# A hand-ordered attention and channel-mix kernel: the plan of steps is placed anew, with other matmuls on zeros

## The chip, the cores and the metric

The kernel runs on one core of one Trainium2 chip. The metric is device time in microseconds (us) of one execution; the time before is the median of three runs. The core has a matrix engine (PE, with its weight loads listed as PEld), a vector engine (DVE), a scalar engine (ACT), a general engine (POOL) and a queue engine (SP); each executes its own instructions strictly in the order in which they were written, and waits on semaphores for the others. Data moves between HBM and on-chip memory by DMA; matmuls write to PSUM, which has eight banks, numbered 0 to 7 in the plan.

## What is computed

Eight batches of eight heads, 576 tokens, head size 64, 32 memory slots. First an attention over a compressed memory, then a channel mix over the 512 joined features, with a shift by one token:

```python
a = softmax(phi)                              # over the 32 slots
k_m = einsum('bhsm,bhsd->bhmd', a, k)
v_m = einsum('bhsm,bhsd->bhmd', a, v)
attn = softmax(q @ k_m.T / sqrt(64))
x = (attn @ v_m) as [B, S, H * D]             # 8, 576, 512
x_prev = x shifted by one token, 0 in front
xk = mu_k * x + (1 - mu_k) * x_prev
xr = mu_r * x + (1 - mu_r) * x_prev
k = maximum(xk @ w_k, 0)                      # 512 -> 1024
out = sigmoid(xr @ w_r) * (k * k @ w_v)       # 1024 -> 512
```

## The kernel before

All of the work is cut into named steps, and a hand-written list, `PLAN` (lines 19 to 84), says in which order they are written out. A loop at line 794 reads it word by word; every word appends the instructions of its step to the queues of the engines concerned. So the list fixes the order on each engine, and the PSUM banks too. A word is `who:step`, then perhaps `/a` or `/d` (ACT or DVE does the copy or the elementwise work) and `@` with the banks that its matmuls take. A step in several stages appears as often as it has stages: `c3:5@2` writes the first matmuls, `c3:5/a` a copy, `c3:5` the last matmuls. The semaphores follow from the data and from the banks: a step that takes a bank waits until the reader of what lay there is done.

The words that matter here:

- `0:` to `7:` are the attention steps of a batch: `exp` of phi, `z` its sums, `kg`, `vg`, `k`, `v`, `kv` the memory products (L319), `h`, `nk`, `nv` their normalization, `tk`, `vt` transposes (L368, L470), `q0`, `q1` the turning of Q (DVE, L388), `s` the scores (L402), `es` their exponentials (ACT, L416, L420), `l`, `r`, `y` the softmax sums, reciprocals and products of batch 0, `fe`, `fs`, `fo`, `w` the same of the later batches, on DVE.
- Batch 0 forms the mixed rows xk and xr directly: `mk`, `mr` (matmuls, L362) and `uk`, `ur`, which unload them to x0T (L545). Its keys are `c0:` (L599, halves a and b, with relu and square as second and third stage), its gates `g:00` to `g:03` (L666).
- Batches 1 to 7 project the memory values through the weights instead: `G02`, `G01`, `Gs0` and so on (L492), `E` to copy them out of PSUM into G (L498), `D` their differences, `d` the differences of the attention between neighbour tokens. A `G0` step reads weights scaled by mu: `m:k0`, `m:k1` (the two halves of w_k) and `m:r0` (w_r) make those (L287). Their keys are `c1:` to `c7:` (L617, L621, L625), relu `r:`, square `s:`, gates `g:10` and so on (L679, L687), `t:` the gates' tanh (L656); `x:` copies the leftover rows of two batches together, `g:e`, `o:e` treat these.
- `o:` is the value product (L757, eight matmuls, one for each block of the 1024 rows), the multiplication by the gate (DVE, L763) and the store. `o:03a` and `o:03b` are its left and right half of the columns, in batch 0 256 each.
- `p:` issues a load on POOL's queue: `p:v:1` is V of batch 1, `p:wk:4-8` a part of the key weights, `p:wv:2-4` the right half of the columns of the value weights, `p:wr` the gate weights.
- `b:2x8@6` writes matmuls on a tile of zeros whose result nobody reads: two of 8 blocks of 64 columns, into bank 6. `WARM` says how many such matmuls stand in front of everything, and how wide.

Stores go to SP's queue; the steps named in `TAIL` spread theirs over SP's and ACT's queue. PE is written so that matmuls of one batch fill the gaps that another's dependencies leave.

Of the kernel before, what the change touches and what calls it, by code (L numbers as in the profile page):

```python
# [16 lines left out]


PLAN = [
# [64 lines left out]
]  # L84

WARM = (36, 2)

PRE = "after: id: q:0a"
TAIL = ("o:73", "o:70", "o:e3", "o:72", "o:71a", "o:71b",)


NJ = 9
# [5 lines left out]
def kernel(  # L98
# [158 lines left out]

    keep_busy(*WARM)

# [579 lines left out]
```

## Time and profile before

| what | value |
|---|---|
| median of three runs | 192.69 us (192.68, 192.69, 194.08) |
| the profiled execution | 194.68 us, its span 192.6 us |
| busy share of PE, DVE, ACT, POOL | 95%, 82%, 79%, 15% |
| mean granted PE clock | 0.988 |
| bytes moved by DMA | 31.91 MB, mean 166 GB/s |

A page of the profile lists busy time by engine, then 40 slices of the span with busy shares and the granted clock of PE in tenths, the DMA queues, the chain of work that ended last (followed back from the last instruction through whatever released each step), and groups of instructions by line. In a group's row stand the line, the engine, the operation, output and input tiles with shapes and the count; behind the bar the busy time in total, the mean ns of one, and then the idle time just before them with what ended it. Instructions that follow each other on an engine overlap a little, so that a group's busy time over its count is less than the mean of one.

### The profile page before, as it was taken

How to read it: one execution, taken by the hardware profiler on the slowest of the kernel's cores; microseconds unless marked ns; L12 is line 12 of the kernel's file. 1: busy time of each engine (PE TensorE's matmuls, PEld its weight loads, DVE VectorE, ACT ScalarE, POOL GpSimd, SP SyncE). 2: the span in 40 equal slices, each digit the busy share in tenths (PEclk: the TensorE clock that was granted, in tenths of full speed). 3: DMA queues.
4: the chain of work that ended last, by engine and by line, in shares of the span. 5: the costliest groups of instructions: out<-in, count | busy, mean ns of one | idle time of the engine just before them, and what ended most of it. 6: DMA issues, size and time to landing. Idle time of an engine off the chain costs nothing.

```text
span 192.6 us, 6111 instructions
## 1 busy us (share of the span) xinstructions
PE 182.2 (95%) x2492; PEld 104.3 (54%) x2492; DVE 158.1 (82%) x341; ACT 151.3 (79%) x360; POOL 29.5 (15%) x45
## 2 busy tenths in 40 slices
PE   7888898999999999999989999999999999999991
PEld 6435663468755466555644565465534753566450
DVE  2147788699988999999997899998999899949441
ACT  2756679797679989999989979978698898587600
POOL 5844242210430140000064000000000000000000
PEclk9999997999999999999999999999999999999998
DMA  5999999999999999992439999724023304413063
GB/s 181 282 203 239 231 207 203 293 241 229 222 231 326 246 225 268 289 192 64 109 33 267 229 241 242 159 49 94 3 58 80 83 12 100 95 44 82 0 163 109
DMA packets 25755, 31.91 MB, mean 166 GB/s; under 512 B 2168, under 2 KB 20352, under 8 KB 25728
## 3 DMA queue, kind: packets, MB, share of 16 engines
q0 software_dynamic: 17888, 20.32, 56.7%
q1 hardware_dynamic: 6272, 8.79, 17.7%
q10 hardware_dynamic: 1568, 2.43, 3.7%
q8 instruction: 19, 0.31, 0.6%
q14 instruction: 8, 0.07, 0.1%
HBM read 38.28 MB, written 9.44 MB: 248 GB/s over the span
## 4 chain that ended last, share of the span: by engine, by line
PE 85%; DMA 5%; ACT 3%; DVE 2%; issue 2%; POOL 1%; POOLq 0%; DVEq 0%; ACTq 0%
PE pv L757 33%; PE pk L625 7%; PE pk L617 7%; PE pb L625 7%; PE gps L492 5%; DMA kv<-in_v_dram 5%; PE pr L687 3%; PE pr L679 3%; PE pb L687 3%; PE kvps L319 3%; PE pr L666 3%; PE pk L599 3%; PE pr L709 2%; PE scps L402 2%; ACT rl L583 1%
## 5 line engine op out<-in xcount | busy, mean ns | idle before, releaser
L757 PE MATMUL pv<-wv,sq 128*128 128x512 bf16 (+3 forms) x296 | 60.8, 350 | 0.0
L757 PEld LDWEIGHTS <-sq 128*128 128x128 bf16 x296 | 27.8, 98 | 26.1 <-issue 3.0
L498 ACT CAST G<-gps 128x512 bf16<-128x512 f32 x63 | 33.6, 618 | 2.1 <-PE gps L492 1.0
L763 DVE SCALAR_TENSOR_TENSOR o<-sg,pv 128x512 f32<-128x512 f32 (+3 forms) x41 | 25.0, 615 | 8.2 <-PE pv L757 7.4
L625 PEld LDWEIGHTS <-G 128*128 128x128 bf16 x224 | 21.5, 98 | 9.1 <-issue 0.6
L625 PE MATMUL pk<-diff,G 128*128 128x288 bf16 x112 | 22.9, 286 | 0.0
L625 PE MATMUL pb<-diff,G 128*128 128x288 bf16 x112 | 22.9, 286 | 0.0
L583 ACT ACTIVATE rl<-pb 128x288 bf16<-128x288 f32 x41 | 17.2, 422 | 6.9 <-PE pb L625 6.7
L583 ACT ACTIVATE rl<-pk 128x288 bf16<-128x288 f32 (+2 forms) x45 | 18.1, 420 | 2.8 <-PE pk L625 1.3
L617 PE MATMUL pk<-atn,G 128*128 128x288 bf16 x112 | 20.0, 286 | 0.0
L621 ACT COPY pb<-pk 128x288 f32<-128x288 f32 x39 | 14.8, 413 | 5.1 <-PE pk L617 1.8
L589 ACT ACTIVATE sq<-rl 128x576 bf16<-128x576 bf16 (+2 forms) x29 | 18.4, 655 | 0.2
L591 DVE TENSOR_TENSOR sq<-rl 128x576 bf16<-128x576 bf16 (+2 forms) x43 | 17.1, 412 | 1.6 <-ACT rl L583 0.9
L501 DVE TENSOR_TENSOR G<-G 128x1024 bf16<-128x1024 bf16 x21 | 14.1, 685 | 0.3
L498 DVE CAST G<-gps 128x512 bf16<-128x512 f32 x21 | 13.8, 683 | 0.6 <-PE gps L492 0.6
L465 DVE TENSOR_TENSOR atn<-e,lz 128x576 bf16<-128x576 bf16 (+2 forms) x18 | 12.1, 683 | 2.5 <-ACT lz L437 2.5
L617 PEld LDWEIGHTS <-G 128*128 128x128 bf16 x112 | 10.4, 98 | 5.6 <-issue 1.1
L656 ACT ACTIVATE sg<-pr 128x512 f32<-128x512 f32 x22 | 13.0, 617 | 0.5 <-PE pr L709 0.5
L585 DVE TENSOR_SCALAR rl<-pk 128x288 bf16<-128x288 f32 (+2 forms) x27 | 11.9, 449 | 1.7 <-PE pk L599 1.2
L388 DVE STREAM_TRANSPOSE qT<-q 128x576 uint32<-128x576 uint32 (+2 forms) x16 | 12.1, 764 | 1.3 <-DMA q<-in_q_dram 1.3
L174 POOL DMA_DIRECT2D kv<-in_v_dram x7 | 5.2, 749 | 37.6 <-PE gps L492 28.5
L299 ACT ACTIVATE em<-ph 128x1152 bf16<-128x1152 f32 (+1 forms) x9 | 9.6, 1075 | 1.6 <-DMA ph<-in_phi_dram 1.6
(99 smaller groups left out, 290.6 us busy)
## 6 DMA issues: line engine op xcount, KB each, us to landing
out_dram<-o SPq DMA_DIRECT2D x51, 128.0 KB, 2.4
ph<-in_phi_dram POOLq DMA_DIRECT2D x7, 576.0 KB, 14.2
kv<-in_k_dram POOLq DMA_DIRECT2D x7, 576.0 KB, 18.5
q<-in_q_dram POOLq DMA_DIRECT2D x7, 576.0 KB, 17.2
kv<-in_v_dram POOLq DMA_DIRECT2D x7, 576.0 KB, 16.3
out_dram<-o SPq DMA_DIRECT2D x26, 64.0 KB, 4.8
k0f<-in_k_dram ACTq DMA_DIRECT2D x2, 576.0 KB, 5.9
wv<-in_moe_w_v_dram POOLq DMA_DIRECT2D x2, 512.0 KB, 18.4
```

What stands on the lines that cost most here:

```text
L388: nc.vector.transpose(dst, src)
L498: return lambda: copier()(g_tile()[:, v, c, GCOLS[i]], st["gps", v, i][c])
L501: return lambda: nc.vector.tensor_sub(g_tile()[:, 1, :, GCOLS[i]], g_tile()[:, 2, :, GCOLS[i]], g_tile()[:, 0, :, GCOLS[i]])
L583: nc.scalar.activation(rl, ps, AF.Relu, scale=HALF ** 0.5)
L589: nc.scalar.activation(dst, rl, AF.Square)
L591: nc.vector.tensor_mul(dst, rl, rl)
L617: nc.tensor.matmul(pa, lhsT=st["G"][:, 2, c, f], rhs=st["at"][:, c, :NP], start=c == 0, stop=False, skip_group_check=True)
L621: copier()(pb, pa)
L625: nc.tensor.matmul(ps, lhsT=st["G"][:, v, c, f], rhs=st["d"][:, kind, c], start=False, stop=c == 1, skip_group_check=True)
L656: nc.scalar.activation(gated[name], ps, AF.Tanh, scale=0.5)
L757: nc.tensor.matmul(pv[:, cols], lhsT=squares, rhs=wv_sb[:, fi, cols], start=(fi == 0), stop=(fi == NF - 1))
L763: nc.vector.scalar_tensor_tensor(o[:, cols], in0=gated[name][:, cols], scalar=1.0, in1=pv[:, cols], op0=AL.add, op1=AL.mult)
```

## The change

All 64 lines of the plan are replaced. The same steps stand in both, apart from the `b:` words; their order, banks and engines differ. Zeros: 36 matmuls in 18 words for 20 in 10. Nearly all of the old ones stand ahead of the keys of batch 0; the new ones also stand within the keys, between the mixing of the gates' rows and the scores of batch 1 (`b:1x6@2`, `b:1x8@7`, `b:1x6@6`) and behind `1:vt`. In front, 10 matmuls of 512 columns take the place of 36 of 128. `p:wv:2-4` is issued ahead of `p:v:1`, `p:q:1` ahead of `p:phi:1` and `p:k:1`. The half values `o:02b`, `o:03b`, `o:01b`, `o:00b` stand ahead of `1:vt` (before, behind it); `m:r0` goes from DVE to ACT, `m:k0` to behind `1:s`. `TAIL` names the last three steps in place of the last six. Nothing but these three constants is changed.

```diff
 PLAN = [
-    "0:exp0 0:mub@0 0:mub 0:c00/a 0:exp1 b:6x8@6 b:1x7@6 0:z@0 p:q:0b 0:c01/a 0:z 0:c11/a 0:c10/a 0:mu@1 p:v:0g 0:q0",
-    "0:kg0@02 b:2x8@6 b:1x7@6 0:kg1 0:h0/d 0:h1/a b:2x8@6 0:tk@0 0:tk p:v:0h 0:q1 p:wk:4-8 p:wk:2-4 p:wk:0-2 0:mu",
-    "p:phi:1 p:k:1 p:q:1 p:wr:0-4 b:1x5@6 0:s0@0234 0:es10 b:2x8@6 0:l10@1 p:v:1 p:wv:2-4 p:wv:0-2 p:phi:2 0:es00",
-    "0:l00@5 0:l10 0:l00 0:r10 0:y10 0:s1@6702 0:r00 0:es01 b:2x8@1 0:vg1@34 0:vg0 0:y00 0:es11 0:nk0 0:l11@0 0:nk1",
-    "0:l01@2 0:l11 0:mk0@6715 0:uk00/d 0:uk01/a 0:nr1 0:l01 0:r01 0:y01 b:2x8@0 b:1x7@0 c0:4a@0 c0:6a@1 0:r11",
-    "c0:5a@2 c0:3a@5 c0:6a/a c0:7a@1 c0:4a/d 0:nr0 0:y11 0:mk1@3406 c0:7a/d m:k0/d 0:uk10/a c0:4a/d c0:0a@7 c0:6a/d",
-    "c0:2a@1 c0:1a@0 c0:0a/d 0:uk11/a c0:4b@3 c0:7a/a c0:7b@4 c0:4b/d 1:exp c0:7b/d c0:4b/a m:k1/d c0:0a/a c0:5b@7",
-    "c0:2a/a c0:5b/a c0:2a/d c0:7b/d c0:0b@3 c0:6b@4 c0:1b@1 c0:5b/d 1:z@6 c0:3b@7 c0:1b/d c0:1b/d c0:6b/a c0:3a/a",
-    "c0:3a/a c0:6b/d c0:2b@5 1:z c0:5a/a p:phi:3 c0:3b/a 0:mr1@1462 c0:0b/a c0:0b/d c0:5a/a p:k:2 0:ur10/a c0:2b/a",
-    "1:k@73 1:q0 1:nk/a c0:3b/d c0:2b/d 0:ur11/a 1:q1 0:mr0@1653 1:tk@7 1:tk c0:1a/a c0:1a/d 1:s@7024 0:ur00/a x:0/a",
-    "1:es0 0:ur01/d g:00@1 1:es1 m:r0/d g:01@3 g:02@5 0:tb g:00 1:fe 1:v@60 1:fs 1:nv/a g:01 g:02 g:03@2 1:vt@0",
-    "1:vt/d 1:G02@06 1:fo g:03 1:G01@47 1:E011/a 1:Gs0@13 1:E020/d p:v:2 o:03b@2 o:03b 1:Es00/a 1:Es01/a 1:E021/a",
-    "1:w0 1:E010/a o:00b@5 1:G00@20 1:E001/a 1:Gs1@13 1:Es11/a 1:w1 1:Gs2@67 1:Es20/a 1:E000/a o:00b o:01a@4",
-    "1:Es21/a 1:d c1:2@5 c1:1@0 c1:0@3 c1:1/a@2 o:01a c1:3@4 o:03a@6 1:D0 c1:2/a@7 c1:2 1:Es10/d o:03a 1:D1 c1:1",
...
-    "c7:1@2 c7:7/a@0 g:70@3 r:700/d g:71/d@6 c7:1/a@5 c7:7 r:701/d s:74/d g:70/d@7 c7:1 r:710/d s:76/a s:70/a g:71",
-    "r:711/a s:71/d t:711 r:770/a g:70 g:e3@2 t:700 t:710 r:771/d t:701 g:e3 s:77/d o:73@1 o:70@5 x:7/a o:73 o:70",
-    "o:e3@0 o:72@1 o:e3 o:72 o:71a@0 o:71a o:71b@1 o:71b",
+    "0:exp0 0:mu@0 0:mub@1 0:mub 0:c01/a 0:c11/d 0:c00/a 0:exp1 b:11x8@6 b:1x7@6 0:z@1 0:z 0:c10/a 0:kg0@23 0:kg1",
+    "0:mu 0:h0/d 0:h1/d b:2x8@6 b:1x7@6 0:tk@0 0:q0 0:tk b:2x8@6 b:1x7@6 0:s0@0123 p:q:0b p:v:0h p:v:0g 0:q1",
+    "p:wk:0-2 p:wk:4-8 p:wk:2-4 0:es10 0:es00 b:3x8@6 0:l10@4 0:l10 0:l00@5 0:l00 0:r10 0:y10 0:s1@6701 0:es11",
+    "0:es01 0:r00 b:2x8@4 b:2x8@5 0:l11@0 0:l01@1 0:vg1@67 0:y00 0:l11 0:l01 p:q:1 b:1x8@5 0:vg0 0:nk1 0:nk0 b:2x8@5",
+    "b:1x7@5 0:mk0@2301 0:uk01/d p:phi:1 0:r11 0:nr1 0:nr0 0:r01 0:y01 0:uk00/a b:2x8@5 c0:1a@4 c0:0a@0 c0:0a/a",
+    "c0:1a/a c0:7a@6 p:k:1 c0:4a@7 c0:5a@0 p:wr:0-4 0:y11 c0:0a/d c0:2a@1 c0:1a/a c0:4a/a c0:6a@2 c0:5a/a c0:6a/a",
+    "0:mk1@0347 c0:3a@5 0:uk11/a m:k1/d c0:6a/a c0:4a/d 0:uk10/d c0:5a/a b:1x5@2 c0:5b@2 c0:3b@0 p:wv:2-4 c0:7a/d",
+    "c0:7a/d c0:3a/d c0:2a/a c0:2b@1 c0:1b@5 1:q1 c0:0b@6 c0:2a/a p:v:1 c0:3a/a c0:3b/a 1:q0 c0:4b@0 1:exp c0:5b/d",
+    "c0:3b/d c0:5b/d p:wv:0-2 c0:7b@2 c0:6b@3 c0:2b/a c0:4b/a 1:z@0 p:phi:2 c0:0b/a c0:2b/d c0:4b/d c0:1b/a c0:6b/a",
+    "c0:0b/d c0:7b/d 1:z c0:6b/d c0:1b/a c0:7b/d x:0/d 0:mr1@1456 1:k@37 0:ur11/d 0:ur10/a b:1x6@2 0:mr0@0215 1:nk/a",
+    "1:tk@3 1:tk 0:ur01/a b:1x8@7 b:1x6@6 1:s@3725 m:k0/d 0:ur00/a 1:es0 1:es1 g:02@0 g:01@1 g:03@2 1:fe 1:fs 0:tb",
+    "g:00@3 o:02b@5 1:fo p:v:2 1:w0 o:03b@7 g:03 g:02 o:02b o:03b o:01b@4 m:r0/a 1:v@60 g:00 p:k:2 p:q:2 g:01",
+    "o:00b@5 p:phi:3 1:nv/a p:v:3 1:w1 1:vt@0 1:vt/d o:01b b:1x8@3 1:G01@06 o:00b 1:G00@71 1:Gs0@42 1:E000/d",
+    "1:E011/a 1:Es00/a 1:Gs1@53 1:d o:01a@6 1:Es01/a c1:1@2 c1:3@4 o:01a 1:Es10/d c1:2@7 c1:0@6 1:Es11/a o:00a@3",
+    "1:E001/a c1:3/a@1 p:k:3 1:E010/a 1:D0 c1:0/d@5 c1:3 c1:2/d@0 o:00a 2:exp c1:0 c1:2 r:100/d r:130/a r:101/a",
+    "s:10/d r:120/a r:131/a c1:6@3 1:D1 o:02a@4 r:121/a c1:6/a@6 c1:5@7 c1:7@0 c1:7/a@1 s:12/d s:13/a c1:6 c1:5/d@5",
...
+    "c7:1/d@2 r:701/d s:70/a o:62 c7:1 c7:3/d@6 g:70@7 c7:2 r:710/a c7:3 g:70/a@3 r:731/a r:720/a g:70 c7:7@0",
+    "r:711/a r:730/d g:71@1 s:71/d g:71/a@6 s:73/a g:e3@2 r:721/d s:72/a c7:7/d@4 c7:7 r:771/d r:770/d s:77/d g:71",
+    "t:711 g:e3 t:700 o:70@4 o:70 o:73@0 x:7/a o:e3@2 o:73 o:72@0 o:e3 o:71a@2 o:71b@4 t:710 t:701 o:72 o:71a o:71b",
 ]
 
-WARM = (36, 2)
+WARM = (10, 8)
 
 PRE = "after: id: q:0a"
-TAIL = ("o:73", "o:70", "o:e3", "o:72", "o:71a", "o:71b",)
+TAIL = ("o:72", "o:71a", "o:71b",)
```

92 rows, old and new, of the table PLAN are left out of this document.

## The prediction, made before the new kernel was run

> **What bounds the kernel now.** I read the page first: busy time by engine, then the slices with the granted clock.
>
> ```profile
> span 192.6 us, 6111 instructions
> ...
> PE 182.2 (95%) x2492; PEld 104.3 (54%) x2492; DVE 158.1 (82%) x341; ACT 151.3 (79%) x360; POOL 29.5 (15%) x45
> ...
> PEclk9999997999999999999999999999999999999998
> ```
>
> PE, the matrix engine, is busy for 95% of the span: the plan is one queue of matmuls with little air. But 95% is an average, and the clock row has a seventh slice that is not full. I then asked for busy time in stretches.
>
> ```profile
> 17.73:31.27 13.54, 11.84 (x229) 8.32 (x228) 10.58 (x33) 10.30 (x30) 5.37 (x7) 1.00 1.22 229
> ```
> ```profile
> 38.00:83.00 45.00, 44.96 (x697) 28.07 (x711) 42.99 (x90) 40.11 (x97) 7.48 (x10) 1.00 1.18 254
> ```
> ```profile
> 27.75:31.17 3.42, 2.75 (x123) 1.59 (x122) 2.48 (x7) 3.42 (x12) 1.47 (x2) 1.00 1.22 205
> 31.17:34.58 3.41, 3.31 (x39) 1.24 (x40) 3.11 (x10) 3.39 (x8) 0.74 (x1) 0.50 1.45 199
> 14.10:17.50 3.40, 2.55 (x94) 1.39 (x94) 2.25 (x7) 2.25 (x10) 0.74 (x1) 1.00 1.33 199
> ```
>
> After the length the columns are busy us of PE, weight loads (PEld), DVE, ACT and POOL, then the clock, the DMA share and GB/s. From 38 us on PE has no gap (44.96 of 45), with DVE (42.99) close behind. Ahead of that lies a prologue paced by batch 0 and by the loads. In 31.17 to 34.58 PE is busy for 3.31 us, but at a clock of 0.50: this follows 3.4 us in which it ran small tiles alone. Third, the chain of waits (start, length, what), cut to the places that the sum needs:
>
> ```profile
> 5.16 9.64 DMA kv<-in_v_dram
> 14.84 0.83 PE kvps L319 x72
> ...
> 16.06 0.67 PE mxps L362 x16
> ...
> 17.73 2.34 PE pk L599 x20
> ...
> 31.27 0.71 PE scps L402 x30
> 31.97 4.00 PE pr L666 x12
> 35.97 0.68 PE kvps L319 x72
> 36.65 0.97 PE pr L666 x4
> ...
> 37.99 0.84 PE gps L492 x24
> 38.83 1.85 PE pv L757 x16
> ...
> 64.73 1.73 PE pv L757 x8
> ```
>
> V of batch 0 lands and starts the mixing (mk0, 16.06), the mixed rows start the keys (17.73), those lead to the scores of batch 1 (31.27), then come gates and the transposed V of batch 1 (vt), and from 37.99 PE is saturated. The real matmul work is the same in both plans. So three things decide: when the new plan saturates PE, how much real work it has done by then, and how well it feeds PE afterwards.
>
> **How the runs stand to this execution.** It took 194.68 us for a span of 192.6, so 2.1 lie around the span. The timed runs are 192.68, 192.69 and 194.08. The half-clock stretch has a price: twelve gate matmuls of 512 columns took 4.00 us, while eight value matmuls of that width take 1.73, so twelve should take 2.59; that is 1.41 lost. The slow timed run is 1.39 above the other two. I read this as: two runs of three had no half-clock stretch, and 192.69 is a time without it. The profiled execution, with it, is 1.99 above the median; the other 0.6 I leave to profiling. What that means for this change: the drop can be removed only from runs that have it, and the median has none.
>
> [...]
>
> **The change, part by part.**
>
> *Ten wide zeros for 36 narrow ones, and a longer row of zeros before the softmax sums of batch 0.*
>
> ```profile
> 5.46 1.87 PE L254 MATMUL idle<-zeros 128*128 128x512 bf16 x7
> ```
>
> Seven zeros of nearly full width take 1.87 us with the end of the last, 0.22 each. Ten end at 1.0+2.2 = 3.2 us, before PE waits for mu anyway (first matmul on it at 4.85). Eleven and one of 7/8 take 2.6 from about 5.5, so end at 8.1; the sums wait for the second exp of phi, which sits one cast (0.67) later in ACT's queue than before, at about 8.6. Cost nothing; were the cover gone, 0.2. In all the plan has 36 zeros for 20: 17,728 columns for 9,856, in front 5,120 for 4,608, so 8,384 columns more, 3.5 us at 0.216 per 512. That is the ceiling if none were covered.
>
> *Ahead of the keys.* The second half of the score exponentials and their sums now stand before V of batch 0, and V's two halves are separate steps with a zero between.
>
> ```profile
> 13.76 0.82 ACT L437 ACTIVATE lz<-lz 128x320 f32<-128x320 f32 x2
> 14.48 0.77 ACT L420 ACTIVATE e<-scps 128x128 bf16<-128x128 f32 x4
> 16.79 0.65 ACT L545 CAST x0T<-mxps 128x256 bf16<-128x256 f32 x2 [0.57 <-PE mxps L362]
> ```
>
> New order on ACT: one reciprocal (0.41), then the four exponentials (0.77): done at 14.95. PE waits for them, does two sums and both halves of V with a zero: 16.1, where before V's sums ended at about 15.6. Behind that, two scalings on DVE, and on PE 0.62 us of zeros that mostly run under them: mk0 at about 16.8 instead of 16.06, keys at 18.4. **Term 1: +0.7** (from 0, if the load of V holds the old order too, to +1.0).
>
> *Keys to the scores of batch 1.* Before: 13.54 us with ACT busy 10.30 and DVE 10.58, so 3 us of air from mutual waits. The new order takes the scaling of the first half of the key weights (m:k0, four by 0.35, 1.4) off DVE and puts it behind the scores; DVE gets two unloads of the mixed rows (0.8 each) and fewer squares, ACT one unload less and more relus. By the steps' counts ACT comes to about 10.8, DVE to 10.0. Following banks and engines word by word I come to 13.0 us. Zeros of 5, 6, 8 and 6 blocks (0.67) lie in waits for an unload or for the normed keys. **Term 2: -0.5**; ends 10.8 (ACT without air, -2.7) and 13.8 (ACT with all the old air, +0.3).
>
> *Loads.* The order on POOL's queue changes.
>
> ```profile
> 30.03 0.74 POOL L174 DMA_DIRECT2D q<-in_q_dram  x1 [1.55 <-DMA wr<-in_moe_w_r_dram]
> 33.12 0.74 POOL L174 DMA_DIRECT2D kv<-in_k_dram  x1 [2.35 <-DMA kv<-in_v_dram]
> ```
>
> Each issue waits for an earlier transfer, so these rows tell landings: gate weights 30.0, V of batch 1 at 33.1, 3.1 us for 576 KB. Half of the value weights (512 KB) put between them lands at about 32.7 and V at 35.8. Values are wanted at 35.5 and V at about 38 in the new order: covered. Q of batch 1 moves ahead of phi and K, which land 3 us later (about 25 and 28); the exponential wants phi at 25.3, K is wanted at 28.7. Cost nothing, with 0.3 to spare on phi; if phi is late ACT waits as long.
>
> *Scores to vt.* Here four half values of batch 0 move ahead of vt: by the row of 16 matmuls in 1.85, 3.7 us of real work done earlier. But m:r0 moves from DVE to ACT, between the gates' tanh steps and the scaled V.
>
> ```profile
> L656 ACT ACTIVATE sg<-pr 128x512 f32<-128x512 f32 x4 | 2.2, 606 | 0.0
> L416 ACT ACTIVATE e<-scps 128x288 bf16<-128x288 f32 x4 | 1.3, 439 | 0.0
> L296 ACT ACT_TABLE_LOAD x1 | 1.3, 1283 | 0.0
> L650 ACT COPY rest<-sq 128x512 bf16<-128x512 bf16 x1 | 0.7, 734 | 0.0
> L353 ACT ACTIVATE vb<-kvps,rz 128x64 bf16<-128x64 f32 x2 | 0.5, 312 | 1.4 <-PE kvps L319 1.4
> ```
>
> No row shows ACT scaling 512 columns of weights. Nearest are the tanh, 0.55 each in a row, and the copy with 0.73: four are 2.2 to 2.9; I take 2.4, nearer to the pipelined row. ACT's queue from the scores: an unload 0.7, exponentials 1.3, table 1.3, four tanh 2.2, m:r0 2.4, V's scaling 0.5, then transpose and copy 0.7: 9.2, with hand-overs 9.4. PE's own work there is 0.4+3.5+3.7+0.7 = 8.3, so ACT sets the end. Before it was 37.99-31.27 = 6.72, without the half clock 5.31. So +4.1, less 3.7 done ahead. **Term 3: +0.4** (-0.7 if PE sets the end, +0.9 with the slow copies). K0's scaling and DVE's sums run beside it; the zero after vt (0.22) runs under its copy.
>
> *Behind saturation.* The tail runs the same six values. Stores of three of them go to SP's queue alone, but eight issues there end before the last value needs one. What differs is the mix:
>
> ```profile
> L498 ACT CAST G<-gps 128x512 bf16<-128x512 f32 x63 | 33.6, 618 | 2.1 <-PE gps L492 1.0 <-PE pr L709 0.8
> ```
>
> In the first 43 us of matmul work from vt I count 94 ACT and 83 DVE steps, 87 and 79 before. At 33.6/63 = 0.53 each that is 3.7 us more on ACT and 2.1 on DVE, in a stretch where they were busy for 40.1 and 43.0 of 45. Most only moves ahead. **Term 4: +0.3** (-0.5, as waits on ACT now on the chain may fall away, to +3.7).
>
> **Sum.** 0.7-0.5+0.4+0.3 = +0.9: 193.6 on the median of 192.69. On the profiled execution: 192.6-1.4+0.9 = 192.1 span, 194.2 with what lies around it.
>
> **Rivals.** *ACT and DVE become the bound in batches 1 to 3.* The filler that fed PE there, four half values, is spent; each c-step needs its G cast and difference. For: DVE 42.99 of 45 already; the counts. Against: PE had no gap with the old mix, and later stretches have slack. It decides once more than 2 us of the added 3.7 plus 2.1 reach PE; with half of it, 2.9: 192.69+0.6+2.9 = 196.2; with 1.7, 195.0. Chance 0.30.
>
> *The half clock belongs to the median after all and the zeros end it, and the keys tighten.* For: zeros stand in the very stretch that preceded the drop. Against: 194.08 beside 192.69. Then 192.69-1.41+0.9 = 192.2; with term 2 at -2.2, 190.5. Chance of that last case, 0.22.
>
> *The zeros don't do it:* the 0.5 us of them (16% of 3.41) are fewer than the 0.6 us of zeros (two of 512 columns, one of 448) in the window 14.10 to 17.50, which kept its clock. If the new plan drops in most runs: 193.6+1.4 = 195.0. Chance 0.05.
>
> **How the numbers follow.** Forecast, near the old time, 0.43. 1% is 1.9 us, about what can be told from no change: below 190.8 is faster, above 194.6 slower. Faster 0.22, same 0.43, slower 0.35. The range goes from 190.6 (term 2 at its good end) to 196.2 (first rival); the likeliest case alone spans 191.9 to 194.6.
>
> **What would show it.** Keys start at 18.1 to 18.7; scores of batch 1 at 30.5 to 32; G of batch 1 at 40 to 42 with ACT full before it; clock 1.00 in the slice at 31 us; PE gaps of over 1 us between 42 and 85 would show the first rival. G of batch 1 before 39.5, or a median difference equal to the lost 1.41, would make me wrong.

## The result, and the profile after

The changed kernel takes 191.67 us, the median of 20 runs (191.32 to 194.22), against 193.16 us for the kernel before on the same chip (20 runs, 192.33 to 194.55). The ratio is 0.9909, 95% interval 0.9884 to 0.9934; it leaves out runs more than 1.5% above a kernel's fastest (two of after), while the medians hold all runs. The forecast was 0.9 us slower; the median came out 1.5 us lower, still within 1%. First the page of after: span, engines, clock by slice.

```profile
span 189.6 us, 6095 instructions
...
PE 183.6 (97%) x2482; PEld 103.4 (55%) x2482; DVE 155.7 (82%) x335; ACT 153.2 (81%) x366; POOL 29.5 (16%) x45
...
PEclk9999999999999999999999999999999999999998
```

The slice at half clock is gone, and the span is 3.0 us shorter. But the profiled execution of before had that stretch and many of its runs don't. So the fair partner is a second profile of before without it (the run `before_again`, the same code; span 191.4). Busy time by stage, columns as in the prediction; the stages are first key to scores of batch 1, scores to G of batch 1, and from there on. First `before_again`, then after:

```profile
17.76:31.50 13.74, 11.84 (x227) 8.32 (x226) 10.66 (x33) 10.27 (x30) 5.29 (x7) 1.00 1.22 228
31.50:36.71 5.21, 4.78 (x120) 2.37 (x123) 4.70 (x12) 5.18 (x13) 1.48 (x2) 1.00 1.43 221
36.71:82.30 45.59, 45.15 (x705) 28.36 (x714) 43.60 (x92) 40.54 (x98) 7.46 (x10) 1.00 1.17 258
```
```profile
18.15:30.18 12.03, 11.90 (x247) 8.37 (x252) 10.61 (x34) 10.29 (x30) 4.00 (x6) 1.00 1.24 230
30.18:38.83 8.65, 8.55 (x154) 5.37 (x155) 7.29 (x14) 7.85 (x17) 1.70 (x3) 1.00 1.28 238
38.83:83.00 44.17, 44.12 (x691) 26.79 (x692) 42.57 (x92) 41.68 (x99) 9.43 (x13) 1.00 1.16 251
```

PE's air in the key stage fell from 1.90 us to 0.13, and the stage from 13.74 to 12.03. Some 0.6 of PE's 11.90 are zeros that fill waits: without them (the run `after_no_late_same_count` below) the stage takes 12.01 with PE busy for 11.27. Behind G PE stays full, with ACT at 41.68 and DVE at 42.57 of 44.17. The chain of waits of after (start, length, what) has the same steps at other times:

```profile
17.26 0.35 PE mxps L362 x16
...
18.15 3.24 PE pk L599 x28
...
30.18 0.41 PE scps L402 x25
30.59 3.56 PE pr L666 x16
34.15 2.62 PE pv L757 x24
36.77 0.68 PE kvps L319 x72
37.45 0.98 PE pv L757 x8
38.43 0.10 PE vtps L470
...
38.83 0.46 PE gps L492 x8
```

The 2.62 and 0.98 of value matmuls (pv) between scores and G are the work done ahead. Stage by stage, after less `before_again`:

| stage | before_again | after | difference | forecast |
|---|---|---|---|---|
| start to first key | 17.76 | 18.15 | +0.39 | +0.7 |
| first key to scores | 13.74 | 12.03 | -1.71 | -0.5 |
| scores to G, less 3.7 done ahead | 5.21 | 8.65 | -0.26 | +0.4 |
| G to end, plus those 3.7 | 154.69 | 150.77 | -0.22 | +0.3 |
| span | 191.4 | 189.6 | -1.80 | +0.9 |

These are two executions out of kernels whose runs spread: 193.45 lies high among the shorter runs of before, 191.42 low among those of after, so that -1.80 is more than the medians show. The start moves most: another profile of the changed kernel (`after_again`) has its first key at 18.94. The three later stages repeat to 0.1 there.

### The profile page after: what moved, and what is told of

It reads as the page before. It is cut to its first block, busy times and chain, and to the rows that moved or that the text cites. A ratio compares the mean times of both kernels' runs of the same rounds, so it can differ in the third digit from the quotient of the medians.

```text
span 189.6 us, 6095 instructions
## 1 busy us (share of the span) xinstructions
PE 183.6 (97%) x2482; PEld 103.4 (55%) x2482; DVE 155.7 (82%) x335; ACT 153.2 (81%) x366; POOL 29.5 (16%) x45
## 4 chain that ended last, share of the span: by engine, by line
PE 91%; DMA 3%; ACT 3%; DVE 1%; issue 0%; ACTq 0%
PE pv L757 34%; PE pk L617 8%; PE pk L625 8%; PE pb L625 7%; PE gps L492 6%; PE pk L599 4%; PE kvps L319 4%; PE pr L687 3%; PE pr L679 3%; PE pb L687 3%; DMA k0f<-in_k_dram 3%; PE idle L254 2%; PE pr L709 2%; PE pr L666 2%; PE scps L402 2%; PE zps L329 1%
## 5 line engine op out<-in xcount | busy, mean ns | idle before, releaser
L498 ACT CAST G<-gps 128x512 bf16<-128x512 f32 x65 | 34.2, 605 | 2.8 <-PE gps L492 2.7
L583 ACT ACTIVATE rl<-pk 128x288 bf16<-128x288 f32 (+2 forms) x48 | 19.0, 416 | 6.0 <-PE pk L625 4.4
L589 ACT ACTIVATE sq<-rl 128x576 bf16<-128x576 bf16 (+2 forms) x30 | 18.9, 645 | 0.6 <-DVE rl L585 0.5
L621 ACT COPY pb<-pk 128x288 f32<-128x288 f32 x39 | 15.8, 421 | 2.6 <-PE pk L617 2.4
L583 ACT ACTIVATE rl<-pb 128x288 bf16<-128x288 f32 x38 | 15.5, 428 | 2.0 <-PE pb L625 1.8
L254 PE MATMUL idle<-zeros 128*128 128x512 bf16 (+3 forms) x46 | 14.1, 411 | 1.3 <-DVE zeros L180 1.0
L498 DVE CAST G<-gps 128x512 bf16<-128x512 f32 x19 | 12.4, 679 | 1.4 <-PE gps L492 1.4
L585 DVE TENSOR_SCALAR rl<-pk 128x288 bf16<-128x288 f32 (+2 forms) x24 | 10.4, 445 | 1.0 <-PE pk L625 0.9
```

The source lines that it names most:

```text
L254: nc.tensor.matmul(ps.rearrange("p (a b) -> p a b", b=64), lhsT=zeros, rhs=zeros[:, :64].unsqueeze(1).to_broadcast([128, blocks, 64]), sta ...
L498: return lambda: copier()(g_tile()[:, v, c, GCOLS[i]], st["gps", v, i][c])
L583: nc.scalar.activation(rl, ps, AF.Relu, scale=HALF ** 0.5)
L589: nc.scalar.activation(dst, rl, AF.Square)
L621: copier()(pb, pa)
```

## The experiments

The table holds all kernels; the ratios are against runs of the kernel before on the same chip, and the stages are those of the profiled execution, in us. What each expectation said stands with its experiment. The profiles of before, `before_narrow` and `before_wide` hold a half-clock stretch, which in the first two lengthens the stage from the scores to G.

| run | median | ratio, 95% | first key | key to scores | scores to G | G to end |
|---|---|---|---|---|---|---|
| before | 193.16 | | 17.73 | 13.54 | 6.72 | 154.61 |
| before_again | 193.48 | 0.997–1.004 | 17.76 | 13.74 | 5.21 | 154.69 |
| before_zeros | 193.42 | 0.996–1.002 | 18.70 | 13.83 | 5.31 | 154.66 |
| before_narrow | 194.50 | 1.001–1.007 | 17.51 | 13.30 | 6.84 | 155.45 |
| before_mk0_narrow | 194.20 | 1.001–1.009 | 17.66 | 13.44 | 5.76 | 155.74 |
| before_wide | 195.56 | 1.001–1.010 | 21.52 | 13.47 | 5.43 | 154.58 |
| before_moved_blocks | 195.84 | 1.005–1.015 | 18.85 | 13.32 | 5.20 | 155.93 |
| after | 191.67 | 0.988–0.993 | 18.15 | 12.03 | 8.65 | 150.77 |
| after_again | 191.70 | 0.987–0.995 | 18.94 | 12.06 | 8.72 | 150.78 |
| after_no_late_zeros | 193.74 | 0.995–1.002 | 18.88 | 11.99 | 8.72 | 152.61 |
| after_no_late_same_count | 191.64 | 0.986–0.994 | 18.15 | 12.01 | 8.72 | 150.82 |
| after_mk0_early | 192.26 | 0.989–0.998 | 18.34 | 12.58 | 8.76 | 150.82 |
| after_halves_late | 197.37 | 1.019–1.028 | 17.99 | 12.04 | 8.73 | 156.54 |
| after_loads_old | 193.28 | 0.994–1.000 | 18.52 | 12.04 | 9.67 | 151.37 |
| after_warm_old | 191.93 | 0.991–1.000 | 20.69 | 12.04 | 8.73 | 150.84 |
| after_short_front | 191.83 | 0.986–0.994 | 19.08 | 12.06 | 8.71 | 150.85 |
| after_solid_front | 192.20 | 0.987–0.995 | 18.85 | 11.88 | 8.78 | 150.79 |

**Do the late zeros earn the gain?** `before_again` is before as it was; `before_zeros` has the three zero words of the new plan at the same places; `after_no_late_zeros` has them taken out.

```diff
 before_zeros
-0:mr0@1653 1:nk/a ... 1:tk@7 1:tk
+b:1x6@5 0:mr0@1653 1:nk/a ... 1:tk@7 b:1x8@2 b:1x6@4 1:tk
 after_no_late_zeros
-b:1x6@2 0:mr0@0215 ... b:1x8@7 b:1x6@6 1:s@3725
+0:mr0@0215 ... 1:s@3725
```

> The kernel before, unchanged, to see how its runs divide and what their granted clock is. Theory A (the half-clock stretch falls on a minority of runs, the median has none): runs near 192.7 us with a mean clock of 0.995 or more, and some near 194.2 with about 0.988; a profile without the stretch has a span near 190.9 and G of batch 1 starts near 36.5 us. Theory B (the stretch is in nearly every run, and the change gains by ending it): the mean clock is about 0.988 at all times, and G starts at 38.0.

> The kernel before with three matmuls on zeros (6, 8 and 6 blocks) between the first memory products of batch 1 and its scores, nothing else. Theory A: the median moves by less than 0.3 us, since most runs had no half-clock stretch; at most the slow group gets smaller. Theory B: 1.4 us less in the median, and a clock of 1.00 at 31 to 35 us.

> The changed kernel without its three zeros between the mixing of batch 0 and the scores of batch 1. Theory A: within 0.3 us of the changed kernel in the median. Theory B: the half-clock stretch comes back, 1.4 us more, mean clock about 0.988.

Put into before, the zeros change nothing that can be measured. Taken out of after they cost 2 us, yet the clock stayed at 1.00 and the key stage at 11.99, so neither theory holds. Behind G 1.84 us are lost, 1.46 of them in one wait that after doesn't have, the second row here; the first has its like in `after_again` (0.49), so it doesn't come from the edit. In the PE timeline (start, length, what, shapes, then the idle time before and its cause; here without a releaser, "issue"):

```profile
16.20 0.21 PE L320 MATMUL kvps<-kv,em 64*32 64x64 bf16 x4 [0.54 <-issue]
67.16 0.34 PE L403 MATMUL scps<-qT,kmT 32*32 32x288 bf16 x12 [1.46 <-issue]
```

(The lines of this kernel count one higher.) The second row is in the scores of batch 3, far from the edit. This raised the question of instruction blocks below. To separate the zeros from their number, `after_no_late_same_count` takes the three out but adds as many instructions in front:

```diff
-b:11x8@6 ... b:1x6@2 0:mr0@0215 ... b:1x8@7 b:1x6@6 1:s@3725
+b:14x6@6 ... 0:mr0@0215 ... 1:s@3725
```

> The changed kernel without its three zeros ahead of the scores of batch 1, and with three matmuls more in the early row of zeros (14 of 384 columns for 11 of 512), so that all later instructions keep their places in the blocks. Without those zeros alone the kernel lost 1.8 us in its later part, 1.46 of it in one wait for instructions in the scores of batch 3. Theory F: that wait is gone, from G to the end 150.8 us, median within 0.4 of the changed kernel, no half clock. Rival (the zeros themselves keep something warm or in step): 152 us or more again.

191.64: all of the gain is there without the late zeros, in 12 runs, with the same 12.01. So the zeros fill holes and don't make the gain; their number matters.

**Does the move of m:k0 shorten the key stage?** `after_mk0_early` puts it back among the keys, ahead of `c0:2a/a`.

```diff
-c0:7a/d c0:3a/d c0:2a/a ... 1:s@3725 m:k0/d
+c0:7a/d c0:3a/d m:k0/d c0:2a/a ... 1:s@3725
```

> The changed kernel with the scaling of the first half of the key weights back on DVE among the keys of batch 0. If taking those 1.2 us off DVE is what shortened the stretch from the first key to the scores from 13.5 to 12.0 us (theory C), it grows by 1.0 to 1.4 again and so does the time. If the shorter stretch comes from the order of the keys, relus and squares alone (theory D), by less than 0.4.

The stage grew by 0.55, to 12.58, between the two expectations, and PE waits for DVE where it didn't:

```profile
26.85 0.84 PE L600 MATMUL pk<-x0T,wk 128*128 128x320 bf16 x5 [0.50 <-DVE rl L586]
```

In before the same move (`before_mk0_narrow`: `m:k0/d` from behind `c0:7a/d` to behind `0:ur01/d`) was made beside a second edit, narrower zeros ahead of the keys, which `before_narrow` has alone:

```diff
-b:6x8@6 ... b:2x8@6 ... b:2x8@6 ... b:2x8@6 ... b:2x8@1 ... b:2x8@0
+b:12x4@6 ... b:4x4@6 ... b:4x4@6 ... b:4x4@6 ... b:4x4@1 ... b:4x4@0
```

> The kernel before with its early zeros of 512 columns (16 of them, ahead of the keys) cut into twice as many of 256: the same time on PE, 32 instructions more ahead of the keys. In every profile of the kernel before PE stands for 0.55 to 0.61 us in the mixing mk1 at the same instruction, about the 700th, and goes on 1.3 to 1.5 us after a block of 256 instructions has arrived. Theory F (PE waits for its own instructions): that boundary moves to another step, the wait in mk1 goes, keys to scores take 13.1 us or less in place of 13.7, and about 0.5 us go from the median unless another boundary falls on a dense step. Rival (the wait is one for data): it stays at mk1, no change.

> The same with the scaling of the first half of the key weights also moved behind the scores of batch 1. If the gain of the stretch from the first key to the scores (13.7 to 12.0 us) is the block boundary (0.6) and that scaling (0.55, as putting it back cost), it takes 12.5 to 12.7 here. If the order of keys, relus and squares is needed for it, over 13.

The key stage of `before_narrow` and of `before_mk0_narrow`:

```profile
17.51:30.81 13.30, 11.91 (x228) 8.23 (x228) 10.29 (x33) 10.07 (x30) 5.56 (x7) 1.00 1.22 229
```
```profile
17.66:31.10 13.44, 11.91 (x228) 8.24 (x227) 9.09 (x29) 10.07 (x30) 5.22 (x7) 1.00 1.22 229
```

There the move gains nothing (13.44 for 13.30), though DVE is busy for 1.2 us less of the stage, and both medians lie above that of before. In the old order something else ended last: PE's waits there are for its own instructions (0.64) and for batch 1's normed keys on ACT and DVE, none for a relu on DVE as above. So 0.55 is the price of m:k0 in the new order; it isn't shown to be a share of what the change gained.

**PE waits for its own instructions.** The row of before that the prediction passed over, and the same place with 16 more matmuls ahead of it (`before_narrow`), each from the PE timeline:

```profile
21.03 0.21 PE L362 MATMUL mxps<-atn,vm 32*64 32x63 bf16 x2 [0.55 <-issue]
```
```profile
20.63 0.36 PE L362 MATMUL mxps<-atn,vm 32*64 32x64 bf16 x18 [0.51 <-issue]
```

Two matmuls of the step mk1 were left behind the wait, then 18: it moved by exactly the 16 added, and so stayed within mk1, where I had expected it to leave the step. It stands at an instruction number, not at a piece of data. The page lists a queue of kind "instruction" with 19 packets and 0.31 MB, so 16 KB each; the trace shows when each landed, and the records of PE's queue (matmuls, weight loads and a few waits for semaphores) can be counted:

```
kernel                wait ends at   PE record   block landed   wait
before                   21.03          705         19.72       0.55
before_again             21.12          705         19.60       0.61
before_narrow            20.63          705         19.12       0.51
before_narrow            83.56         2744         82.00       0.60
before_wide              18.39          449         17.02       2.12
after_no_late_zeros      16.20          449         14.78       0.54
after_no_late_zeros      67.16         2237         65.73       1.46
after_again              16.27          449         14.84       0.49
```

705 is 449 and 256; 2241 would be 449 and seven times 256, 2753 nine times (the counts of 2237 and 2744 hold 4 and 9 matmuls fewer than weight loads, which are records missing from the trace). Eight more such waits, of 0.23 to 0.86 us, stand at 449, 705, 2241 and 2744 in `before_zeros`, `before_mk0_narrow`, `before_moved_blocks` and `after_warm_old`; one wait marked "issue", of 0.21 in `before_narrow`, stands at none of these places. In every row of the table PE takes up the block 1.3 to 1.6 us after it landed; it had come to the first record of it sooner than that. In after it comes to record 705 at 22.5, 2.9 us after the block landed at 19.65, and doesn't wait. In the dense steps here (mk1, V's products, scores) the waits took 0.23 to 2.12 us. `before_moved_blocks` puts it to the test: zeros of nearly the same columns, cut so that 68 more instructions stand ahead of the keys, the real work untouched.

```diff
-WARM = (36, 2)      b:6x8@6 b:1x7@6 ... b:2x8@6 ... b:1x5@6
+WARM = (46, 2)      b:16x3@6 b:2x4@6 ... b:4x4@6 ... b:2x3@6
```

> The kernel before, with the zeros ahead of the keys cut into narrower matmuls of about the same total width, so that some 34 more matmuls (68 instructions with their weight loads) stand ahead of the keys; the real work and its order are as before. Theory (PE waits for a block of its own instructions where a dense step crosses the block's end): the wait of 0.55 to 0.61 us in mk1 goes elsewhere or goes away, first key to scores of batch 1 takes 13.0 to 13.2 us for 13.5 to 13.8, later parts unchanged unless the block's end falls into another dense step. Rival (the wait belongs to mk1 itself, to its data or its banks): the wait stays in mk1 and the stretch takes 13.5 to 13.8. Median 193.0 or less by the theory, 193.5 by the rival.

```profile
15.18 0.27 PE L402 MATMUL scps<-qT,kmT 32*32 32x128 bf16 x12 [0.85 <-issue]
21.31 0.61 PE L599 MATMUL pk<-x0T,wk 128*128 128x256 bf16 x4 [0.55 <-issue]
21.85 0.49 PE L362 MATMUL mxps<-atn,vm 32*64 32x256 bf16 x32
63.14 0.41 PE L492 MATMUL gps<-mwk,vT 64*32 64x512 bf16 x6 [0.70 <-issue]
```

mk1 (the 32 matmuls at 21.85) has no wait any more: the rival falls. I had expected the wait to go away, and it did not: it stands at records 449, 705 and 2241 again, now in the scores of batch 0, in the keys just ahead of mk1, and in G. So the stage still has 0.55 in it and takes 13.32, and the kernel is 1% slower than before with the same real work: the first key comes 1.1 later (the 0.85, and 46 narrow zeros that take 5.09 us, where the 36 take 4.02 in `before_again`), and 1.2 is lost behind G, 0.70 of it in the wait at 63.14; the other 0.5 I did not trace.

**The work done ahead of vt.** `after_halves_late` puts the four half values behind vt again, `after_loads_old` exchanges `p:wv:2-4` and `p:v:1`.

```diff
 after_halves_late
-g:00@3 o:02b@5 1:fo ... o:03b@7 g:03 g:02 o:02b o:03b o:01b@4 ... 1:vt@0 1:vt/d o:01b
+g:00@3 1:fo ... g:03 g:02 ... 1:vt@0 1:vt/d ... 1:Gs0@42 o:02b@5 o:03b@3 ... o:02b o:03b o:01b@7
 after_loads_old
-p:wv:2-4 ... p:v:1
+p:v:1 ... p:wv:2-4
```

> The changed kernel with the four half values of batch 0 put back behind vt of batch 1. Filler theory: ACT sets the start of G (its queue doesn't shorten), so G starts within 0.5 us of the old 38.8, PE idles some 3 us ahead of it, and the time grows by 2.5 to 3.7. Rival (PE sets it): G starts at 35.2 and the time stays within 0.5.

> The changed kernel with V of batch 1 issued ahead of the right half of the value weights, as before the change. Load theory: those weights land some 3 us later, at about 36, and the half values, first in PE's queue behind the gates at 34.1, wait 1.5 to 2.5 us; the time grows by as much, and the wait may bring the half clock. Rival (the order is without weight, since the transfers share the queues anyway): within 0.4.

`after_halves_late` costs 5.8 us behind G, more than either theory had, while G itself starts at 38.76, as in after (38.83). So the 3.7 us of matmuls were free where they stand. Moved away, they leave 2.1 more than their own time, and the window rows, just before G and from G on, show where most of it goes:

```profile
35.00:38.87 3.87, 1.30 (x82) 0.85 (x89) 2.59 (x4) 3.16 (x7) 2.18 (x3) 1.00 1.25 285
38.87:42.29 3.42, 3.42 (x35) 1.74 (x28) 0.86 (x2) 1.66 (x3) 0.04 (x1) 0.50 1.20 205
```

From G on PE is busy all the time, at a clock of 0.50; each of the six timed runs of this kernel has the same mean clock, 0.991. At 0.50 those 3.42 us hold 1.71 us of full-speed work, so 1.71 is lost there, an estimate from the row; the remaining 0.4 stays open. It follows a stretch in which PE did little, 1.30 busy of 3.87. With the loads in the old order (`after_loads_old`) PE waits for the value weights, 0.81 where 1.5 to 2.5 was expected, and G comes 1.0 later within its stage, without a half clock:

```profile
35.41 2.79 PE L757 MATMUL pv<-wv,sq 128*128 128x256 bf16 x24 [0.81 <-DMA wv<-in_moe_w_v_dram]
```

**The front.** `before_wide` and `after_warm_old` exchange the zeros in front, `after_short_front` halves the width of the eleven, `after_solid_front` takes away the pause between the ten and the eleven.

```diff
 before_wide:        -WARM = (36, 2)   +WARM = (10, 8)
 after_warm_old:     -WARM = (10, 8)   +WARM = (36, 2)
 after_short_front:  -b:11x8@6         +b:11x4@6
 after_solid_front
-0:exp0 0:mu@0 0:mub@1 0:mub ... b:11x8@6 b:1x7@6 ... 0:c10/a 0:kg0@23 0:kg1 0:mu ... 0:tk
+0:exp0 ... b:11x8@6 b:1x7@6 ... 0:c10/a 0:kg0@23 0:kg1 0:mu@0 0:mub@1 0:mu ... 0:tk 0:mub
```

> The kernel before with only the front of the change: 10 matmuls on zeros of 512 columns for 36 of 128. It has 52 instructions fewer ahead of everything, so the block boundary that stopped PE in mk1 comes 26 matmuls later, some 24 into the keys behind mk1. Theory F (instruction blocks): no wait in mk1, keys to scores 13.0 to 13.2 us in place of 13.5 to 13.8, the lowest runs 0.4 to 0.6 under those of the kernel before, unless a later boundary lands badly. Rival (the zeros in front matter only through the clock): the wait in mk1 stays.

> The changed kernel with 36 narrow matmuls on zeros in front again. Theory W (full-width zeros bring the clock up at the first chance, narrow ones, held to one per 98 ns by their weight loads, sometimes miss it): of the runs more lie 1.0 to 2.5 us above the lowest than the 4 of 20 of the changed kernel, and the median rises by 0.2 to 1. Rival (the front is covered by the load of mu and phi): no difference beyond 0.3.

> The changed kernel with the row of 11 early zeros half as wide (256 columns), the count of instructions kept. Where the clock rises only at about 10 us, the full row costs PE 2.6 us ahead of the keys. Theory S (start of the clock): the lower runs stay at 191.3 to 191.9, the upper ones fall from 194.2 to about 193. Rival (the wide row is what brings the clock up): more late runs, median 0.5 or more higher.

> The changed kernel with the matmuls of mu and mub (and the first memory product kg1 and its copy) put behind the sums of phi, so that the ten wide zeros in front and the row of eleven follow each other without the pause for mu. Theory (a late rise of the clock makes the upper group of runs, and the pause causes it): no run above 193, all in one group at 191.0 to 191.9, clock risen by 7.8 us in the profile. Rival (the rise comes late for another reason): about one run in five still at 193.5 to 194.3, as in the control.

> The changed kernel itself, once more, on the chip of the two others: median 191.5 to 191.9, about one run in five at 193.5 to 194.3.

The runs of after lie in two groups: of 32, 24 lie at 191.3 to 192.3 and 8 at 193.7 to 194.2. Those of before do too: in the two rows of 20 that the result compares, 13 lie at 192.3 to 193.6 and 7 at 194.1 to 194.6. Group by group the gain is uneven: the medians of the lower groups differ by 1.25 us (192.77 and 191.52), those of the upper ones by 0.15 (194.28 and 194.13). The zeros in the PE timeline of after and of `after_warm_old`, whose profiled execution (194.07) is one of its five long ones of 12:

```profile
0.99 3.74 PE L254 MATMUL idle<-zeros 128*128 128x512 bf16 x10 [0.99 <-DVE zeros L180]
...
5.37 2.96 PE L254 MATMUL idle<-zeros 128*128 128x512 bf16 x12
```
```profile
0.99 4.02 PE L254 MATMUL idle<-zeros 128*128 128x128 bf16 x36 [0.99 <-DVE zeros L180]
6.20 4.68 PE L254 MATMUL idle<-zeros 128*128 128x512 bf16 x12
```

The same twelve take 2.96 us or 4.68. In the second PE ran at half speed until 9.74 us, when the trace's first mark of the clock stands; in after that mark is at 3.88, and the ten wide zeros start 0.427 us apart ahead of it and 0.216 behind it. The page of after shows full clock (9 tenths or more) ahead of this mark, and the mean clock of the second execution is 0.996 in spite of the late mark, so it can't be seen there. The narrow zeros show it too: in before they start 0.107 us apart up to the mark at 3.86 and 0.056 behind it. So the 98 ns of the theory above (36 zeros in 3.53 us) is a mean over two clocks, and not the pace of the weight loads. `after_warm_old` itself settles nothing: five long runs of 12 against 8 of 32, and a median 0.2 to 0.3 higher. The long row of zeros turns a late rise into a late first key, 20.69 for 18.15. The short front met a late rise too (10.12 us), with its first key at 19.08; three of its seven runs lie at 192.4, four at 191.0 to 191.8. In the unbroken front the mark is at 4.99, and the 22 zeros are one row:

```profile
0.99 7.07 PE L254 MATMUL idle<-zeros 128*128 128x512 bf16 x22 [0.99 <-DVE zeros L180]
```

Neither of these two has a long run in 7 each; at 8 of 32, 14 runs without one would have a chance of 0.75^14, about 2%. Together that supports the late rise as the cause of the upper group; that the pause for mu causes the late rise is not shown, since seven runs are few. Neither front beats after on the median: the runs of `after_solid_front` (192.05 to 192.97) lie above the expected 191.0 to 191.9; its first key, at 18.85, is no later than that of `after_again`, so the reason is open. In `before_wide` ten wide zeros alone make before no faster, against the expectation: its lowest run is 193.26, that of before beside it 192.22. Its profile, of one of its longest runs, has a late rise (9.71), the wait of 2.12 in V's products, a first key at 21.52, and a stretch at half clock from 19.95 to 23.37. No wait for instructions falls into its key stage, which takes 13.47 all the same, but 1.85 us of that at half clock; so it can't tell what the wait in mk1 was worth.

## Why the prediction was wrong, and where it was right

**Term 2 failed: "I come to 13.0 us", -0.5.** It took 12.03, -1.71 against `before_again` and -1.51 against the profile that the prediction read, and this alone turns the sign (0.7-1.7+0.4+0.3 = -0.3). I followed banks and engines word by word and kept most of the 3 us of "air from mutual waits" as a property of the stage. The traces say which waits of PE went. First `before_again`, where these rows hold 1.77 of PE's 1.90 us of idle time in the stage, then the new order without its zeros (`after_no_late_same_count`):

```profile
21.12 0.22 PE L362 MATMUL mxps<-atn,vm 32*64 32x63 bf16 x2 [0.61 <-issue]
27.31 0.70 PE L599 MATMUL pk<-x0T,wk 128*128 128x320 bf16 x4 [0.53 <-ACT rl L583]
29.35 0.89 PE L362 MATMUL mxps<-atn,vm 32*64 32x256 bf16 x3
30.49 0.41 PE L362 MATMUL mxps<-atn,vm 32*64 32x256 bf16 x13 [0.25 <-ACT kbd L344]
31.50 0.48 PE L402 MATMUL scps<-qT,kmT 32*32 32x288 bf16 x32 [0.38 <-DVE kmT L372]
```

```profile
28.53 0.66 PE L362 MATMUL mxps<-atn,vm 32*64 32x256 bf16 x16
29.35 0.28 PE L368 MATMUL ktps<-identity,kbd 128*128 128x128 bf16 x2 [0.16 <-ACT kbd L344]
30.16 0.48 PE L402 MATMUL scps<-qT,kmT 32*32 32x288 bf16 x32 [0.52 <-DVE kmT L372]
```

The waits for the normed keys (kbd, ACT) and for their copy (kmT, DVE) are still there. Two are gone: 0.61 for a block of PE's instructions and 0.53 for a relu on ACT. The remaining 0.57 is busy time of PE, 11.84 against 11.27 for the same real work: matmuls that run spread out, as the three of the mixing at 29.35, which take 0.89 us, while all 16 take 0.66 in the new order. The wait for instructions stands in all three profiles of the kernels with before's order and count up to there (before, `before_again`, `before_zeros`) and in none of after's key stage; but it could not be taken out alone, since in the versions of before that I made it came back nearby or the profile was spoiled otherwise. That it's worth its full 0.6 of the stage is therefore read from the trace, not shown by an experiment; nor is it shown which moves in the plan ended the other two parts. My end of 10.8 was out of reach, since PE's own work takes 11.27. Nor did the counts behind it come true: 10.8 for ACT and 10.0 for DVE were 10.29 and 10.61, as before. The lower end of the range, 190.6, doesn't follow from term 2's good end either: 192.69+0.7-2.7+0.4+0.3 is 191.4, close to the time measured.

**The row was there.** PE's idle time marked "issue" in mk1 stands in the trace of before. I read the chain and the stage sums and did not ask why PE stood still there with nothing to wait for.

**Terms 1, 3 and 4 were each too high, by 0.3 to 0.7.** Together they account for 1.5 of the 2.7 us between the sum and the two profiles, term 2 for 1.2. Keys start at 18.15, just inside 18.1 to 18.7 (18.94 in `after_again`, so term 1 is within the spread). G was to start at 40 to 42 and started at 38.83 (39.72 in `after_again`); before 39.5 was the prediction's own sign of being wrong. ACT's queue as the setter was right: its scaling of V ends at 38.23 and transpose, copy and G follow at once. Its sum was 9.4 and came to 8.65:

```profile
29.86 0.67 ACT L545 CAST x0T<-mxps 128x256 bf16<-128x256 f32 x2
...
34.30 2.55 ACT L285 ACTIVATE mwr<-wr,mu 128x512 bf16<-128x512 bf16 x4
...
37.70 0.53 ACT L353 ACTIVATE vb<-kvps,rz 128x64 bf16<-128x64 f32 x2
```

The four copies of m:r0 took 2.55 for the 2.4 taken; but the unload that I counted at 0.7 behind the scores' start began 0.32 before it, and neighbours overlap by about 0.1 each (those of m:r0 take 0.72 and start 0.61 apart). The 3.7 of value work ahead of vt was right to a tenth (2.62 and 0.98). The loads: V and the value weights came in time, as worked out, and the exchange is needed (1.6 us without it). The first rival is refuted: PE has 0.05 us of air in 44.17, with ACT busy for 41.68 of it and DVE for 42.57.

**The front was priced wrongly, without harm in the median.** "Ten end at 3.2": they end at 4.7, since I took the price of a zero from the row at 5.46, after the clock had risen. The ten took 3.74 us in all, 0.37 each for the 0.22 of that row. "Cost nothing" holds where the clock rises early. Where it rises late the first key of `after_warm_old` comes 2.5 us later (20.69 for 18.15), about the distance of the two groups of after (2.6); the upper one holds a quarter of the runs.

**How I read the three runs was half right.** A half-clock stretch occurs in some runs of before: of the 107 timed beside the experiments, 20 have a mean clock of 0.988 to 0.990, and the profiled execution with the stretch has 0.988. No run of after shows it: none of the 32 has less than 0.995. But 194.08 need not have been such a run: on one chip, runs of before at 194.04 (mean clock 0.995) and at 194.71 (0.989) lie side by side. The first kind is probably the late rise: the profile of `before_zeros`, 194.57 at 0.996, has its first mark of the clock at 10.06 and its first key at 18.70. The "other 0.6" that I left to profiling isn't that: a run's time is its span and, in nearly all runs, 1.7 to 2.2 more, profiled or not. The second rival, that zeros end the half clock and so shorten the median, is refuted as a cause: without the late zeros none of 12 runs of after shows it either (0.994 or more in both kernels without them).

## What to carry to other kernels

Ask of every stage with air on the bounding engine what ended each pause, and take "issue" on that engine seriously: here its place followed the instruction count, an edit far ahead, even of idle matmuls, moved waits of 0.23 to 2.12 us from step to step, and a control with the same count was needed to tell. Look for an order that keeps real work ready in front of a chain on another engine: here 3.7 us of value matmuls stood ahead of G, which started at 38.83 with them and at 38.76 without. Group the runs by span and mean clock before a difference between two of them is put down to a cause.

## What the runs showed of the hardware that was not expected

PE's waits for 16 KB blocks at records 449, 705, 2237 or 2241, and 2744, up to 2.12 us, which end 1.3 to 1.6 us after the block landed. The half speed at the start (wide zeros 0.427 us apart, then 0.216), which the clock row shows as full clock, and which lasts until 3.86 to 10.12 us with matmuls issued from 0.99 us on. And the half clock behind a stretch that is thin in matmuls (1.30 busy of 3.87) in the profile of `after_halves_late`, with a mean clock of 0.991 in all six of its runs.
